# A linear-attention and two-MLP kernel: orders planned forward and backward in rounds, w2's loads held back, the last block's output tiles finished in turn

## The chip, the cores and the metric
The kernel runs on one core of a Trainium2 chip. The core has a matrix engine (TensorE, PE in the profile, with its weight loads as PEld), VectorE (DVE), ScalarE (ACT), GpSimd (POOL, unused here) and SyncE (SP), which issues every DMA of this kernel. The metric is the device time of one execution in microseconds, the median over runs.

## What is computed
```python
# q, k, v, f_logit: (4, 8, 768, 48); heads are joined to x: (3072, 384)
f = 1.0 / (1.0 + np.exp(-f_logit))
for t in range(S):
    state = f[:, :, t, :, None] * state + np.einsum('bhd,bhe->bhde', k[:, :, t], v[:, :, t])
    y[:, :, t] = np.einsum('bhd,bhde->bhe', q[:, :, t], state)
# MLP 1: w_in (384, 2048), w_out (2048, 384)
h = x @ w_in
x = (h * np.clip(h + 3.0, 0.0, 6.0) / 6.0) @ w_out
# MLP 2: weights of its own, same shapes
h = x @ w_in
out = (h * np.tanh(np.log1p(np.exp(h)))) @ w_out
```

## The kernel before
**Tiling.** The scan is done in 24 units `u` (4 batches of 6 chunks of 128 tokens): per unit the decay logs are summed (`sum_up`, matmuls with the triangle `tri`, in units 0 to 7; a scan on VectorE, L278, later), `k` is transposed (`turn`: tile `m`), `scores` are formed (tile `a`), masked by VectorE, and `values` and `outer` multiply them and update the state `st`. A unit ends with two halves of x, `xh` and `xl`: every fp32 value is carried as a rounded part and a rest, and a product takes three matmuls (high by high, low by high, high by low; `passes`).

The MLPs work on 12 blocks of 512 tokens, six for MLP 1 and six for MLP 2. A block has 16 hidden tiles f. `hidden` records for each: nine matmuls of 128x512 into a bank `h` (MLP 2 uses `h`, `a` and `m` in turn), here called H of f; the chain on VectorE and ScalarE that makes `gh` and `gl` (MLP 1: `g`, `gh`, `gl`; MLP 2: a longer chain with tiles `k` and `q`); and nine output matmuls, three for each of the tiles o0, o1, o2 (O of f). Those three banks collect over all 16 f; after f=15 ScalarE, VectorE and ScalarE copy them out and SP stores them, 256 KB each. Attention units of block j+1 are woven between the tiles of block j; units 0 to 3, and most of the preparation, stand ahead of the first hidden matmul (the head).

**Weights.** They come as 64-bit words (`raw`, 768 KB a tile). `stream` makes fp32 of them with two ScalarE passes (`we<-raw`, `raw<-raw`) and two VectorE passes (L220, L222); `weight` splits them into `wh` and `wl`. Those of MLP 1 are converted in the head and in block 0. Those of MLP 2 (w2) are converted later, stored to DRAM (`w<-we`) and read back at the start of MLP 2.

**Order.** Every operation is recorded in a `Plan` with an engine, a cost and a rank, and `emit` sets the order: it walks forward in planned time, and each engine that comes free takes the ready operation of lowest rank. The rank is a due time in hidden tiles (`i` = 16 x block + f). SP's DMAs have planned places of the same kind. In the last block the hidden matmuls of f from 2 up get a rank lower by `TAIL_LEAD` (6), so that they run ahead of the output matmuls. Where the plan leaves TensorE a gap ahead of the first hidden matmul, `emit` fills it with `warm`: matmuls of `cap` into a bank that nobody reads, as many pieces of 128 columns as fit, plus six at the very start.

Of the kernel before, what the change touches and what calls it, by code (L numbers as in the profile page):

```python
# [23 lines left out]
NF = DFF // 128  # L24
# [19 lines left out]
GAP = 0.28  # L44
HOLD, TAIL_LEAD = 14, 6
WE = 2
W2_AT = 40
W2_GAP = 3.5
SPANS = ((0, D), (HB, R))
# [24 lines left out]
class Op:  # L74
    __slots__ = ("eng", "cost", "lat", "rank", "fn", "deps", "after", "seq", "start", "end", "left", "outs", "ready")


class Plan:
# [10 lines left out]
    def op(self, eng, cost, rank, fn, r=(), w=(), lat=0.0):  # L89
        o = Op()  # L90
        o.eng, o.cost, o.lat, o.rank, o.fn, o.seq = eng, cost, lat, rank, fn, len(self.ops)
        o.deps, o.after = set(), set()
# [20 lines left out]

    def emit(self, filled, limit, unit, warm):
# [8 lines left out]
        for o in self.ops:  # L123
            o.outs, o.left, o.ready = [], 0, 0.0
        for o in self.ops:
            o.deps.discard(o)
            o.after -= o.deps | {o}
            for d in o.deps | o.after:
                d.outs.append(o)
            o.left = len(o.deps) + len(o.after)  # L130
        wait = {o.eng: [] for o in self.ops}
        free = dict.fromkeys(wait, 0.0)
        for o in self.ops:
            if not o.left:
                wait[o.eng].append(o)
        order = []
        while any(wait.values()):
            now, eng = min((max(free[e], min(o.ready for o in c)), e) for e, c in wait.items() if c)
            o = min((o for o in wait[eng] if o.ready <= now), key=lambda o: (o.rank, o.seq))
            wait[eng].remove(o)  # L140
            if eng == filled:
                limit = min(limit, now) if o.rank >= 1 else limit
                if free[eng] and free[eng] + unit < now < limit:
                    order.append(int((now - free[eng]) / unit))
            o.start, o.end = now, now + o.cost
            free[eng] = o.end
            order.append(o)
            for d in o.outs:
                t = o.start if d in o.after or o in d.after and o not in d.deps else \
                    o.end + o.lat + (GAP if d.eng != eng else 0.0)  # L150
                d.ready = max(d.ready, t)
                d.left -= 1
                if not d.left:
                    wait[d.eng].append(d)
# [681 lines left out]
```

## Time and profile before
| | |
|---|---|
| time, median of 3 runs | 894.73 us (893.9 to 894.84) |
| profiled execution | 895.67 us, span 893.9 us |
| TensorE busy | 881.0 us (99%) |
| VectorE busy | 668.7 us (75%) |
| ScalarE busy | 561.5 us (63%) |
| mean granted TensorE clock | 0.997 |

The span runs from the first to the last instruction of the profiled execution; the execution's own time has 1.77 us around it. Busy times are sums over the instructions of an engine. In the timeline a row gives start, duration, engine, line, operation, tiles (out<-in), shapes and how many instructions were joined; what ended an idle time before the row stands behind it in brackets. Matmuls overlap in the pipeline, so starts say more than durations.

### The profile page before, as it was taken

The numbers are of one execution on the slowest core, as the hardware profiler recorded it, in microseconds if no ns is written. First come the engines' busy times: TensorE is split into PE (matmuls) and PEld (weight loads), VectorE is DVE, ScalarE is ACT, GpSimd is POOL, SyncE is SP. The second block draws the span as 40 slices with busy tenths as digits, with TensorE's granted clock in tenths as the row PEclk, the third lists the DMA queues.
The fourth block names the chain that finished last, engine by engine and source line by source line (L and its number), as shares of the span: only waits on it lengthen the run. The fifth ranks groups of instructions, "written<-read, shape, count | busy, mean of one in ns | idle before, by whom it ended". The sixth has DMA issues, their size and how long they took to land.

```text
span 893.9 us, 15680 instructions
## 1 busy us (share of the span) xinstructions
PE 881.0 (99%) x6341; PEld 722.0 (81%) x6341; DVE 668.7 (75%) x1045; ACT 561.5 (63%) x978; POOL 0.2 (0%) x4
## 2 busy tenths in 40 slices
PE   9999989999999999999999999999999999999997
PEld 6878868888888888888888888888888888888785
DVE  4898999778777555653565977888878888785894
ACT  6898787667646454433545766666666667664773
POOL 0000000000000000000000000000000000000000
PEclk9999999999999999999999999999999999999999
DMA  8766656867544222100323200100100100000001
GB/s 267 237 200 225 205 192 210 267 209 234 192 133 130 65 65 76 60 25 1 120 92 102 76 1 12 59 1 24 48 0 24 48 1 18 30 1 1 36 1 40
DMA packets 32465, 83.29 MB, mean 93 GB/s; under 512 B 3712, under 2 KB 7040, under 8 KB 32384
## 3 DMA queue, kind: packets, MB, share of 16 engines
q1 hardware_dynamic: 32384, 82.20, 28.9%
q8 instruction: 52, 0.85, 0.4%
q14 instruction: 29, 0.24, 0.1%
HBM read 66.45 MB, written 15.73 MB: 92 GB/s over the span
## 4 chain that ended last, share of the span: by engine, by line
PE 93%; ACT 2%; DVE 2%; DMA 1%; issue 0%; ACTq 0%
PE o L200 45%; PE h L200 30%; PE a L200 12%; PE m L200 7%; DMA raw<-w 1%; PE m L300 1%; ACT we L187 1%; ACT wh L187 0%; DVE we L220 0%; ACT raw L187 0%; DVE b L278 0%; DVE A L290 0%; PE m L400 0%; DVE we L222 0%; ACT vk L187 0%
## 5 line engine op out<-in xcount | busy, mean ns | idle before, releaser
L200 PE MATMUL o<-gh,wh 128*128 128x512 f32 x570 | 225.1, 395 | 0.0
L200 PE MATMUL o<-gl,wh 128*128 128x512 f32 x570 | 222.3, 390 | 0.7 <-DVE gl L203 0.7
L200 PE MATMUL o<-gh,wl 128*128 128x512 f32 x570 | 222.0, 389 | 0.0
L200 PE MATMUL h<-xh,wh 128*128 128x512 f32 x402 | 159.0, 396 | 2.1 <-DVE g L517 2.1
L200 PE MATMUL h<-xh,wl 128*128 128x512 f32 x402 | 157.3, 391 | 0.3 <-DVE wl L203 0.3
L200 PE MATMUL h<-xl,wh 128*128 128x512 f32 x402 | 157.0, 391 | 0.0
L200 PEld LDWEIGHTS o<-gh,wh 128*128 128x128 f32 x570 | 107.0, 188 | 24.2 <-issue 0.4
L200 PEld LDWEIGHTS o<-gh,wl 128*128 128x128 f32 x570 | 107.0, 188 | 22.6
L200 PEld LDWEIGHTS o<-gl,wh 128*128 128x128 f32 x570 | 107.1, 188 | 22.5 <-DVE gl L203 1.1
L517 DVE SCALAR_TENSOR_TENSOR g<-g,h 128x512 f32<-128x512 f32 x96 | 65.6, 684 | 79.1 <-ACT g L187 79.0
L187 ACT ACTIVATE g<-h,small 128x512 f32<-128x512 f32 x96 | 65.8, 686 | 82.3 <-PE h L200 69.7
L187 ACT ACTIVATE gh<-q 128x512 fp32r<-128x512 f32 x94 | 59.3, 631 | 79.8 <-DVE q L206 75.0
L203 DVE TENSOR_TENSOR gl<-g,gh 128x512 fp32r<-128x512 f32 x96 | 66.1, 689 | 33.4 <-ACT gh L187 33.1
L200 PEld LDWEIGHTS h<-xh,wh 128*128 128x128 f32 x402 | 75.6, 188 | 18.7 <-DVE g L517 2.7
L200 PEld LDWEIGHTS h<-xh,wl 128*128 128x128 f32 x402 | 75.7, 188 | 17.1 <-DVE wl L203 1.0
L200 PEld LDWEIGHTS h<-xl,wh 128*128 128x128 f32 x402 | 75.8, 188 | 15.2
L187 ACT ACTIVATE q<-k,small 128x512 f32<-128x512 f32 x96 | 69.4, 723 | 28.8 <-DVE k L525 25.1
L206 DVE TENSOR_TENSOR q<-q,k 128x512 f32<-128x512 f32 x96 | 66.0, 688 | 24.9 <-ACT q L187 23.5
L187 ACT ACTIVATE gh<-g 128x512 fp32r<-128x512 f32 x96 | 60.2, 627 | 35.3 <-DVE g L517 35.2
L203 DVE TENSOR_TENSOR gl<-q,gh 128x512 fp32r<-128x512 f32 x94 | 64.7, 688 | 9.2 <-ACT gh L187 8.5
L187 ACT ACTIVATE k<-k 128x512 f32<-128x512 f32 x96 | 59.6, 625 | 17.6 <-DVE k L522 17.4
L525 DVE SCALAR_TENSOR_TENSOR k<-k 128x512 f32<-128x512 f32 x96 | 65.3, 684 | 0.7 <-ACT k L187 0.7
(140 smaller groups left out, 1164.8 us busy)
## 6 DMA issues: line engine op xcount, KB each, us to landing
raw<-w SPq DMA_DIRECT2D x32, 768.0 KB, 5.2
v<-vs SPq DMA_DIRECT2D x16, 512.0 KB, 3.8
w<-we SPq DMA_DIRECT2D x16, 384.0 KB, 2.7
raw<-w SPq DMA_DIRECT2D x16, 384.0 KB, 3.0
k<-kt SPq DMA_DIRECT2D x24, 224.0 KB, 4.3
q<-qt SPq DMA_DIRECT2D x24, 224.0 KB, 3.6
x<-o SPq DMA_DIRECT2D x18, 256.0 KB, 2.1
f<-x SPq DMA_DIRECT2D x18, 256.0 KB, 2.6
```

The source lines that it names most:

```text
L187: lambda: nc.scalar.activation(out=out(), in_=in_(), func=func, **k), r, w)
L200: nc.tensor.matmul(**k)
L203: dve(n, rank, lambda: nc.vector.tensor_tensor(out=out(), in0=a(), in1=b().bitcast(F32), op=ALU.subtract), r, w)
L206: dve(n, rank, lambda: nc.vector.tensor_tensor(out=out(), in0=a(), in1=b(), op=ALU.mult), r, w)
L300: nc.tensor.transpose(ztv()[:, p, :], k3()[:, p, :], ident[0:R, 0:R])
L517: dve(n, rank, lambda: nc.vector.scalar_tensor_tensor(out=gg(), in0=gg(), scalar=6.0, in1=zn(), op0=ALU.min, op1=ALU.mult), (g, z), (g,))
L525: dve(n, rank, lambda: nc.vector.scalar_tensor_tensor(out=ee(), in0=ee(), scalar=2.0, in1=ee(), op0=ALU.add, op1=ALU.mult), (e,), (e,))
```

## The change
1. `forward` is the old walk. `backward` walks from the planned end back and gives each operation its latest start, which becomes its rank in the next forward walk. They alternate for six rounds, and the plan with the earliest end is kept; operations are emitted by planned start.
2. Fillers in gaps that begin before 8 us of planned time are counted at twice the length, so fewer are placed.
3. w2's raw loads wait for a hidden tile: tile f for the hidden tile number 22 + 3.5 f (22 is f=6 of block 1).
4. In the last block the lead of the hidden matmuls grows in steps from 6/14 to 6. The output matmuls of f from 12 up are ranked by output tile: all of o0 first, then o1. o2 is collected up to f=13 and copied to SBUF (`rest`); f=14 and 15 are collected in two halves of 256 columns in the two `h` banks, VectorE adds `rest` to each, and each half is stored by itself (128 KB).

```diff
 GAP = 0.28
+COLD = 8.0
+ROUNDS = 6
 HOLD, TAIL_LEAD = 14, 6
+APART = 4
...
 W2_AT = 40
 W2_GAP = 3.5
+W2_FROM = 22
...
+    def forward(self):
+
+        wait = {o.eng: [] for o in self.ops}
+        free = dict.fromkeys(wait, 0.0)
+        for o in self.ops:
+            o.ready, o.left = 0.0, len(o.deps) + len(o.after)
+            if not o.left:
+                wait[o.eng].append(o)
+        while any(wait.values()):
+            now, eng = min((max(free[e], min(o.ready for o in c)), e) for e, c in wait.items() if c)
+            o = min((o for o in wait[eng] if o.ready <= now), key=lambda o: (o.rank, o.seq))
+            wait[eng].remove(o)
+            o.start, o.end = now, now + o.cost
+            free[eng] = o.end
+            for d in o.outs:
+                d.ready = max(d.ready, o.end + o.lat + (GAP if d.eng != eng else 0.0) if o in d.deps else o.start)
+                d.left -= 1
+                if not d.left:
+                    wait[d.eng].append(d)
+        return max(o.end for o in self.ops)
...
+    def backward(self):
+
+        end = max(o.end for o in self.ops)
+        wait = {o.eng: [] for o in self.ops}
+        free = dict.fromkeys(wait, end)
+        for o in self.ops:
+            o.ready, o.left = end, len(o.outs)
+            if not o.left:
+                wait[o.eng].append(o)
+        while any(wait.values()):
+            now, eng = max((min(free[e], max(o.ready for o in c)), e) for e, c in wait.items() if c)
+            o = max((o for o in wait[eng] if o.ready >= now), key=lambda o: (o.end, o.seq))
+            wait[eng].remove(o)
+            o.rank = now - o.cost
+            free[eng] = o.rank
+            for d in o.deps | o.after:
+                d.ready = min(d.ready, o.rank - d.lat - (GAP if d.eng != eng else 0.0) if d in o.deps else o.rank + d.cost)
+                d.left -= 1
+                if not d.left:
+                    wait[d.eng].append(d)
...
         for o in self.ops:
-            o.outs, o.left, o.ready = [], 0, 0.0
-        for o in self.ops:
             o.deps.discard(o)
             o.after -= o.deps | {o}
+            o.outs = []
+        for o in self.ops:
             for d in o.deps | o.after:
                 d.outs.append(o)
-            o.left = len(o.deps) + len(o.after)
...
-        order = []
...
-            if eng == filled:
-                limit = min(limit, now) if o.rank >= 1 else limit
-                if free[eng] and free[eng] + unit < now < limit:
-                    order.append(int((now - free[eng]) / unit))
...
+        best = None
+        for i in range(ROUNDS + 1):
+            end = self.forward()
+            if best is None or end < best[0]:
+                best = end, [(o, o.start, o.end) for o in self.ops]
+            if i < ROUNDS:
+                self.backward()
+        for o, o.start, o.end in best[1]:
+            pass
+        order, free = [], {}
+        for o in sorted(self.ops, key=lambda o: (o.start, o.seq)):
+            if o.eng == filled:
+                limit = min(limit, o.start) if o.mlp else limit
+                if o.eng in free:
+                    slow = unit * (2 if free[o.eng] < COLD else 1)
+                    if free[o.eng] + slow < o.start < limit:
+                        order.append(int((o.start - free[o.eng]) / slow))
+                free[o.eng] = o.end
             order.append(o)
...
-    def stream(w, f, rank, name=None):
+    def stream(w, f, rank, name=None, after=()):
         raw = new("raw", [128, 2 * DM * (2 if wide else 1)], 2, U32)
-        dma(rank - 3, raw, lambda: w[f].bitcast(U32), (), (raw,), 128 * 2 * DM * (8 if wide else 4), name)
+        dma(rank - 3, raw, lambda: w[f].bitcast(U32), after, (raw,), 128 * 2 * DM * (8 if wide else 4), name)
...
-    pso = {}
+    pso, halves, rest = {}, [], []
...
-        pe(9 * (0.0135 + n / 2400), i - TAIL_LEAD * tail, run, [("w", f, 0), ("w", f, 1), *x_keys(ph, j, 0), *x_keys(ph, j, 1)], (z,))
+        pe(9 * (0.0135 + n / 2400), i - (TAIL_LEAD * (f - NF + HOLD + 1) / HOLD if tail else 0), run, [("w", f, 0), ("w", f, 1), *x_keys(ph, j, 0), *x_keys(ph, j, 1)], (z, ("h", i)))
...
         if f == 0:
             pso[0] = [bank(f"o{m}", [128, 512], 1) for m in range(KC)]
         for m in range(KC):
-            zo = pso[0][m]
-
-            def run(m=m, zo=zo):
-                for t, (a, b) in enumerate(passes):
-                    mm(out=zo()[:, 0:n], lhsT=ww[f][a][:, DM + m * 128:DM + (m + 1) * 128], rhs=gn[b](),
-                       start=(f == 0 and t == 0), stop=(f == NF - 1 and t == 2))
-
-            pe(3 * (0.0135 + n / 2400), i + 1.5 + m * 0.01, run, (("w", f, 0), ("w", f, 1), *gs, *((zo,) if f else ())),
-               (zo,))
-            if f == NF - 1:
+            cut = tail and m == KC - 1 and f >= NF - 2
+            for i0, (s0, s1) in enumerate(((0, n // 2), (n // 2, n)) if cut else ((0, n),)):
+                if cut and f == NF - 2:
+                    halves.append(bank("h", [128, 512], 2))
+                zo = halves[i0] if cut else pso[0][m]
+                begin = f == NF - 2 if cut else not f
+                done = f == NF - 1 or tail and m == KC - 1 and f == NF - 3
+
+                def run(m=m, zo=zo, s0=s0, s1=s1, begin=begin, done=done):
+                    for t, (a, b) in enumerate(passes):
+                        mm(out=zo()[:, s0:s1], lhsT=ww[f][a][:, DM + m * 128:DM + (m + 1) * 128], rhs=gn[b]()[:, s0:s1],
+                           start=(begin and t == 0), stop=(done and t == 2))
+
+                at = i - f + NF - APART + 1.5 + (m * APART + f + 2 * i0) * 0.01 if tail and f >= NF - APART else i + 1.5 + m * 0.01
+                pe(3 * (0.0135 + (s1 - s0) / 2400), at, run, (("w", f, 0), ("w", f, 1), *gs, *(() if begin else (zo,))), (zo,))
+                if not done:
+                    continue
                 scale = 1.0 / 6.0 if ph == 1 else 1.0
-                o = new("o", [128, 512], 3)
-                on = lambda o=o: o()[:, 0:n]
-                zi = lambda zo=zo: zo()[:, 0:n]
-                if m == 1:
+                o = new("k" if cut else "o", [128, 512], 3)
+                on = lambda o=o, s0=s0, s1=s1: o()[:, s0:s1]
+                zi = lambda zo=zo, s0=s0, s1=s1: zo()[:, s0:s1]
+                if cut:
+                    dve(s1 - s0, i, lambda on=on, zi=zi, s0=s0, s1=s1: nc.vector.tensor_tensor(
+                        out=on(), in0=zi(), in1=rest[0]()[:, s0:s1], op=ALU.add), (zo, rest[0]), (o,))
+                elif m == 1:
                     dve(n, i, lambda on=on, zi=zi: nc.vector.tensor_scalar(out=on(), in0=zi(), scalar1=scale,
                                                                            scalar2=None, op0=ALU.mult), (zo,), (o,))
                 else:
                     act(n, i, on, zi, AF.Copy, (zo,), (o,), scale=scale)
+                if f < NF - 1:
+                    rest.append(o)
+                    continue
                 dst = x1_d[j] if ph == 1 else out_v[:, :, t0:t0 + n]
-                dma(i, lambda m=m, dst=dst: dst[:, m, :], on, (o,), (("x1", j, m) if ph == 1 else ("out", j, m),),
-                    128 * n * 4)
+                dma(i, lambda m=m, dst=dst, s0=s0, s1=s1: dst[:, m, s0:s1], on, (o,),
+                    (("x1", j, m) if ph == 1 else ("out", j, m, s0),), 128 * (s1 - s0) * 4)
 
 
     P.op("act", 1.3, -99, lambda: nc.scalar.preload_act_table_set("natural_log_exp_and_others"))
@@ -603,7 +657,7 @@
         for f in range(NF):
             hidden(1, j, f, 16 * j + f)
     for f in range(NF):
-        key, src = stream(w2, f, W2_AT + W2_GAP * f)
+        key, src = stream(w2, f, W2_AT + W2_GAP * f, after=(("h", int(W2_FROM + W2_GAP * f)),))
```

In the planned order this moves instructions at three places. First, TensorE at the head. `o_147` is the bank of the fillers, `o_164<-tri,f` are unit 0's sums, `m<-ident,k` a `turn` and `a<-q,k` its `scores`. Before, from the start:

```order
L200 MATMUL o_147<-cap 112x128
L200 MATMUL o_147<-cap 112x512 x3
L200 MATMUL o_147<-cap 112x128 x2
L200 MATMUL o_164<-tri,f 112x128 x4
L200 MATMUL o_147<-cap 112x512 x2
L200 MATMUL o_147<-cap 112x128 x2
L400 MATMUL m<-ident,k 128x112 x4
```

and after:

```order
L241 MATMUL o_147<-cap 112x128
L241 MATMUL o_147<-cap 112x512
L241 MATMUL o_147<-cap 112x128 x3
L241 MATMUL o_164<-tri,f 112x128 x4
L241 MATMUL o_147<-cap 112x512
L241 MATMUL o_147<-cap 112x128
L441 MATMUL m<-ident,k 128x112 x4
```

The first batch shrinks from 1,920 to 1,024 columns and the second from 1,280 to 640. Further on, up to the first hidden matmul (`h<-xh,wh_96`), 13 pieces of 128 columns become 6. Just ahead of that matmul stand before (`h<-g,v` belongs to unit 3, `m<-tri,f` to unit 5):

```order
L200 MATMUL h<-g,v 32x128 x5
L200 MATMUL m<-tri,f 112x128 x4
L200 MATMUL o_147<-cap 112x512
L200 MATMUL o_147<-cap 112x128
L200 MATMUL h<-xh,wh_96 128x512
```

and after:

```order
L241 MATMUL h<-g,v 32x128 x5
L441 MATMUL m<-ident,k 128x112 x4
L241 MATMUL a<-q,k 128x128 x8
L241 MATMUL o_147<-cap 112x128 x3
L241 MATMUL h<-xh,wh_96 128x512
```

Unit 4's `turn` and `scores`, which stood behind the nine matmuls of H0, now stand ahead of them. Before, H0, H1, unit 4's `outer` and `values` and H2 come before O0, the first output matmuls; after, H0, H1, unit 4's `outer` and `values`, and then O0.

Second, VectorE at the start of block 1 (`b<-cap,f` is a unit's scan, `we` a conversion pass, `st` and `A<-a,tri` follow a unit's scores). Before:

```order
L278 SCALAR_TENSOR_TENSOR b<-cap,f 112x512
L206 TENSOR_TENSOR k<-k,f 112x512
L290 TENSOR_TENSOR A<-q,b 64x512
L290 TENSOR_TENSOR A<-q,b 48x512
L203 TENSOR_TENSOR gl<-g,gh 128x512
L206 TENSOR_TENSOR k<-k,f 112x512
L290 TENSOR_TENSOR A<-q,b 64x512
L290 TENSOR_TENSOR A<-q,b 48x512
L220 SCALAR_TENSOR_TENSOR we<-we,raw 128x768
L329 TENSOR_TENSOR st<-st,a 112x192
L339 TENSOR_TENSOR A<-a,tri 64x256 x4
L517 SCALAR_TENSOR_TENSOR g<-g,h 128x512
```

and after:

```order
L319 SCALAR_TENSOR_TENSOR b<-cap,f 112x512
L247 TENSOR_TENSOR k<-k,f 112x512
L244 TENSOR_TENSOR gl<-g,gh 128x512
L331 TENSOR_TENSOR A<-q,b 64x512
L331 TENSOR_TENSOR A<-q,b 48x512
L247 TENSOR_TENSOR k<-k,f 112x512
L558 SCALAR_TENSOR_TENSOR g<-g,h 128x512
L331 TENSOR_TENSOR A<-q,b 64x512
L331 TENSOR_TENSOR A<-q,b 48x512
L244 TENSOR_TENSOR gl<-g,gh 128x512
L370 TENSOR_TENSOR st<-st,a 112x192
L380 TENSOR_TENSOR A<-a,tri 64x256 x4
```

The conversion pass is gone from there, and one `g` stands ahead of the second unit's work and of the masks.

Third, TensorE's end (wh_124 to wl_127 are the weights of f=14 and 15; `f` and `A` hold the last two `gh` and `gl`). Before, the three output tiles in turn for each f:

```order
L200 MATMUL o_8200<-f,wh_124 128x512 x2
L200 MATMUL o_8200<-f,wl_125 128x512
L200 MATMUL o_8207<-f,wh_124 128x512 x2
L200 MATMUL o_8207<-f,wl_125 128x512
L200 MATMUL o_8214<-f,wh_124 128x512 x2
L200 MATMUL o_8214<-f,wl_125 128x512
L200 MATMUL o_8200<-A,wh_126 128x512 x2
L200 MATMUL o_8200<-A,wl_127 128x512
L200 MATMUL o_8207<-A,wh_126 128x512 x2
L200 MATMUL o_8207<-A,wl_127 128x512
L200 MATMUL o_8214<-A,wh_126 128x512 x2
L200 MATMUL o_8214<-A,wl_127 128x512
```

and after:

```order
L241 MATMUL o_8162<-A,wh_126 128x512 x2
L241 MATMUL o_8162<-A,wl_127 128x512
L241 MATMUL o_8190<-f,wh_124 128x512 x2
L241 MATMUL o_8190<-f,wl_125 128x512
L241 MATMUL o_8190<-A,wh_126 128x512 x2
L241 MATMUL o_8190<-A,wl_127 128x512
L241 MATMUL h<-f,wh_124 128x256 x2
L241 MATMUL h<-f,wl_125 128x256
L241 MATMUL h<-A,wh_126 128x256 x2
L241 MATMUL h<-A,wl_127 128x256
L241 MATMUL h<-f,wh_124 128x256 x2
L241 MATMUL h<-f,wl_125 128x256
```

The last two rows (f=15 of the second half) are left out. o0 is complete 18 matmuls (6 full ones and 12 halves) before the end, o1 12 halves before it.

In the same block H6 moves: H1 and H6 use the one bank `m`, and between them stand 18 matmuls before (H5 and O0) and 81 after.

## Rows read from the trace of the kernel before
**Rows 1.** The page, part 1: busy us, share of the span, instructions

```profile
PE 881.0 (99%) x6341; PEld 722.0 (81%) x6341; DVE 668.7 (75%) x1045; ACT 561.5 (63%) x978; POOL 0.2 (0%) x4
```

**Rows 2.** The chain that ended last: start us, us, what

```profile
871.37 16.33 PE o L200 x72
```

**Rows 3.** TensorE's waits: us in total, times, longest

```profile
PE h L200 <- DVE g L517: 2.1, 2, 1.9
...
PE h L200 <- DVE wl L203: 0.3, 1, 0.3
```

**Rows 4.** Timeline of TensorE, head

```profile
1.59 6.41 PE L200 MATMUL o<-cap 112*112 112x128 f32 x12 [1.59 <-DVE small L573]
7.84 1.04 PE L200 MATMUL o<-tri,f 128*112 128x128 f32 x8
8.71 2.32 PE L200 MATMUL o<-cap 112*112 112x512 f32 x8
10.87 0.55 PE L400 MATMUL m<-ident,k 112*128 112x112 f32 x4
...
33.00 0.48 PE L200 MATMUL h<-xh,wh 128*128 128x512 f32 x1
...
36.72 0.50 PE L200 MATMUL h<-xh,wh 128*128 128x512 f32 x1
```

**Rows 5.** Timeline of ScalarE and VectorE, head

```profile
4.03 0.58 ACT L187 ACTIVATE f<-f 128x448 f32<-128x448 f32 x1
8.97 0.60 ACT L187 ACTIVATE f<-o 112x512 f32<-112x512 f32 x1 [4.37 <-PE o L200]
...
9.70 0.69 DVE L206 TENSOR_TENSOR k<-k,f 112x512 f32<-112x512 f32 x1 [7.56 <-ACT f L187]
```

**Rows 6.** Windows of 20 us: busy us by engine, granted clock, DMA

```profile
120.00:140.00 20.00, 18.14 (x196) 14.46 (x195) 18.19 (x32) 15.37 (x36) 0.00 (x0) 0.91 0.62 202
...
60.00:80.00 20.00, 20.00 (x163) 16.22 (x162) 18.65 (x26) 16.67 (x26) 0.00 (x0) 1.00 0.61 202
```

**Rows 7.** Timeline of TensorE, start of block 1

```profile
117.09 0.50 PE L200 MATMUL o<-gl,wh 128*128 128x512 f32 x1 [0.74 <-DVE gl L203]
...
122.72 0.50 PE L200 MATMUL h<-xh,wh 128*128 128x512 f32 x1 [1.86 <-DVE g L517]
```

**Rows 8.** Timeline of VectorE, start of block 1

```profile
109.63 0.96 DVE L220 SCALAR_TENSOR_TENSOR we<-we,raw 128x768 uint32<-128x768 uint32 x1 [0.55 <-ACT raw L187]
...
118.96 0.96 DVE L220 SCALAR_TENSOR_TENSOR we<-we,raw 128x768 uint32<-128x768 uint32 x1
119.84 0.35 DVE L329 TENSOR_TENSOR st<-st,a 112x192 f32<-112x192 f32 x1
120.22 1.73 DVE L339 TENSOR_TENSOR A<-a,tri 64x256 f32<-64x256 f32 x4
121.98 0.69 DVE L517 SCALAR_TENSOR_TENSOR g<-g,h 128x512 f32<-128x512 f32 x1
```

**Rows 9.** Timeline of TensorE, last block

```profile
836.18 0.50 PE L200 MATMUL m<-xh,wh 128*128 128x512 f32 x1 [1.35 <-DVE q L206]
```

**Rows 10.** Timeline at the end, and the DMA issues of that stretch (KB, median us to landing)

```profile
887.30 0.39 PE L200 MATMUL o<-A,wl 128*128 128x512 f32 x1
887.72 0.60 ACT L187 ACTIVATE o<-o 128x512 f32<-128x512 f32 x1 [0.76 <-PE o L200]
...
out_dram<-o SPq DMA_DIRECT2D x3, 256.0 KB, 3.8
```

**Rows 11.** Timeline of SP's queue: stores of converted w2 tiles, first and last of 14

```profile
140.13 0.34 SPq L193 DMA_DIRECT2D w<-we  x1
...
255.72 0.42 SPq L193 DMA_DIRECT2D w<-we  x1
```

**Rows 12.** The page, part 5: a group of weight loads (busy, mean ns)

```profile
L200 PEld LDWEIGHTS o<-gh,wh 128*128 128x128 f32 x570 | 107.0, 188 | 24.2 <-issue 0.4
```

**Rows 13.** The page, part 6: stores of x between the MLPs (KB, us to landing)

```profile
x<-o SPq DMA_DIRECT2D x18, 256.0 KB, 2.1
```

More of the change, by code (lines that the diff above doesn't have):

```diff
@@ L74 @@
 class Op:
-    __slots__ = ("eng", "cost", "lat", "rank", "fn", "deps", "after", "seq", "start", "end", "left", "outs", "ready")
+    __slots__ = ("mlp", "eng", "cost", "lat", "rank", "fn", "deps", "after", "seq", "start", "end", "left", "outs", "ready")
 class Plan:
@@ L91, in op @@
         o.eng, o.cost, o.lat, o.rank, o.fn, o.seq = eng, cost, lat, rank, fn, len(self.ops)
+        o.mlp = rank >= 1
         o.deps, o.after = set(), set()
@@ L123, in emit @@
         for o in self.ops:
-            o.outs, o.left, o.ready = [], 0, 0.0
-        for o in self.ops:
             o.deps.discard(o)
             o.after -= o.deps | {o}
+            o.outs = []
+        for o in self.ops:
             for d in o.deps | o.after:
                 d.outs.append(o)
-            o.left = len(o.deps) + len(o.after)
[L131 to L135, printed above, removed]
-        order = []
[L137 to L140, printed above, removed]
-            if eng == filled:
-                limit = min(limit, now) if o.rank >= 1 else limit
-                if free[eng] and free[eng] + unit < now < limit:
-                    order.append(int((now - free[eng]) / unit))
-            o.start, o.end = now, now + o.cost
-            free[eng] = o.end
-            order.append(o)
[L148 to L154, printed above, removed]
+        best = None
[16 more added lines that the diff above has]
+                free[o.eng] = o.end
+            order.append(o)
         for o in order:
```

## The prediction, made before the changed kernel ran
> **What bounds the kernel now.** I read the page's busy times first: TensorE is busy 881.0 of 893.9 us [rows 1], so the kernel is TensorE's, and a gain can come from three things only: its idle time, work that need not be done (the filler matmuls on `cap`), and matmuls that run at the slower clock. The chain that ended last says the same at the end: 72 output matmuls in 16.33 us [rows 2], 0.2268 us from start to start. That is the price of every 128x512 matmul here; 3,456 of them are 784 us and are untouched.
>
> Then TensorE's waits: six lines, the first for VectorE's `g` and the last for `wl` [rows 3], all for VectorE or ScalarE and none for a DMA. They sum to 6.6 us, a little over half of the 12.9 us of idle time; the rest is the end of the span, where TensorE has nothing left. The timeline then tells where each wait stands:
>
> - Head. TensorE starts at 1.59 with six fillers (3 of 512 columns, 3 of 128) and reaches unit 0's `tri` sums at 7.84; after these come two more long fillers, and the first `turn` starts at 10.87, the first hidden matmul (H0) at 33.00 [rows 4]. ScalarE had `f` ready at 4.03 + 0.58 = 4.61 and then waited 4.37 us for TensorE [rows 5]: a filler that counts as busy held up the chain.
> - Block 0. VectorE is busy 18.65 of 20 us at 60 to 80 us [rows 6]: little room.
> - Start of block 1. Two waits for `g`, 2.1 us together [rows 3], the longer (1.86) at 122.72, and one of 0.74 for `gl` at 117.09 [rows 7], and the granted clock is 0.91 of full over 120 to 140 us [rows 6]. The levels are 1.2 and 2.4 GHz, so 20 x 0.09 x 2 = 3.6 us ran at the lower one and cost half of that. VectorE is not slow there; its queue holds the wrong things: two passes of w2's conversion (0.96 us each, the first at 109.63) stand before one `g`, a third at 118.96 before the masks, and the `g` that frees the bank for the next hidden tile comes last, at 121.98 [rows 8].
> - Last block. H6 waits 1.35 us for bank `m`, which VectorE's multiply into `q` frees [rows 9].
> - Tail. The last matmul starts at 887.30, its eviction at 887.72 takes 0.60, and the store issued then takes about 3.8 us [rows 10]. That is 6.2 us from the last matmul's end to the span's.
>
> **The sum.** It is made against the profiled run (895.67 us, of which 1.77 lie around the span).
>
> *Head.* The first batch of fillers loses 512 + 384 − 896 columns: before it is 1,920 columns in 7.84 − 1.59 = 6.25 us, after 1,024, so 3.33 us: `tri` starts at 4.9 instead of 7.84, just after `f` (4.61). It runs at the lower level then, 2 x 0.87 us, to 6.7. ScalarE's and VectorE's steps behind it gave `k` at 9.70 + 0.69 = 10.39 [rows 5], 1.68 after `tri`'s end at 8.71; so they give it at 8.3 to 8.4, and the first `turn` starts at about 8.5 instead of 10.87. The second batch of fillers is 640 columns instead of 1,280 (2.16 us at the full level); begun at 6.7, it ends at about 8.3 if the clock rises at 7.84 as before. That is −2.4. Between there and H0 the fillers shrink from 13 to 6 pieces of 128 columns, each 2.16/10 = 0.216 us: −1.5. But unit 4's `turn` and `scores` now stand ahead of H0. They take 36.72 − 33.00 − 9 x 0.2268 = 1.7 us [rows 4]. So H0 starts near 30.7 (−2.3), and H1, which no longer has them before it, 3.9 us earlier. Bounds: −3 (their inputs come late) to −5 (all fillers were in the way). **−3.9.**
>
> *New wait at O0.* TensorE now reaches O0 two hidden tiles after H0, with unit 3's sums between them: about 36.9. VectorE has between unit 3's `xl` (about 30.3) and `gl` of f=0: five conversion or `wl` passes at 0.88 from start to start (118.96 to 119.84 [rows 8]), two masks, `g`, `gl` and `xl` of about 0.6, and two small ones of 0.35: some 7.8 us, so about 38.1. Wait 1.2, less the old wait for `wl` (0.3 in the list, 0.4 by starts): **+0.8**, bounds 0 and +2 (a wait as long as the 1.86 of [rows 7]).
>
> *Start of block 1.* No w2 conversion stands there any more, and `g` is moved ahead of the masks, whose scores come from TensorE itself. What TensorE lost: 2.1 + 0.7 by the list, and 1.8 by the lower clock: **−4.6**, bounds −2.8 (the waits go, the lower clock stays) and −5.2 (each wait's start-to-start gap is 0.1 to 0.25 longer than its number).
>
> *Conversions in blocks 1 to 4.* Each of the 16 tiles brings two VectorE passes and two ScalarE passes, one tile every 3.5 hidden tiles (3.5 x 18 x 0.2268 = 14.3 us of matmuls, so the passes take an eighth of it). In before 14 of the 16 tiles were stored between 140 and 256 us [rows 11], and no wait of TensorE stands between 130 and 830 us: there is cover. Where a unit's scan and masks fall together with a conversion, a short wait can come back: **+0.3**, bounds 0 and +4.6 (all of what block 1 loses now).
>
> *Last block.* In the order of after, 81 matmuls (18 us) instead of 18 (4.1 us) stand between H1 and H6, the two users of bank `m`; VectorE needs under 6 us for H1's chain. **−1.4**, bounds −1.0 and −1.5. The stepwise leads also let 57 matmuls (12.9 us) stand between the last hidden tile and its first output matmul, where 63 (14.3 us) stood; no output matmul of the last block waited before, so I count nothing, and +1.4 as the bound.
>
> *Tail.* o0 and o1 are finished 2.7 and 1.4 us before the last matmul (12 halves, 6 x 0.2268). The last eviction has 256 columns a row: VectorE's four 256-wide masks take 1.73, so 0.43 each [rows 8] against 0.60: −0.17. The 12 half matmuls cost at least half of 0.2268, and at most 0.188, the length of a weight load [rows 12]: nothing to +0.9. Eight `tri` pieces of 128 columns start every 0.11 us [rows 4], so the weight load isn't the bound even there; I take 0.12, +0.1. The last store has 128 KB. Stores of 256 KB that go out at other times land in 2.1 us [rows 13], the last three, which overlap, in 3.8. With o0 and o1 out of the way I take 2.6: −1.2. **−1.3**, bounds +0.9 (the store as slow as before) and −1.9.
> The Trainium skill (DMA: Bandwidth & Descriptors, "Anatomy of one DMA") speaks against this: about 2.0 us of a transfer are fixed, and only bytes at 436 GB/s scale, which would make halving worth 0.3 us and the tail −0.4 if overlap cost nothing. The 2.1 against 3.8 us for one size say that overlap does cost here, so the measurement decides for now; by the rule alone the sum would be 0.9 smaller.
>
> Sum: −3.9 + 0.8 − 4.6 + 0.3 − 1.4 − 1.3 = −10.1, so 885.6 for a profiled run. The median of the timed runs is 0.94 below the profiled one, which makes **884.6**. Its own range, with terms erring independently, is 882 to 887.3.
>
> **Rivals.**
> *B: block 0 eats the head.* VectorE is 93% busy there [rows 6] and does the same conversions in the same block. If its work from H0 to the end of block 0 can't start earlier, the 3.1 us of head and O0 are given back as waits inside block 0: −7.0, 887.7. For it: the busy share. Against: conversions for block 0 do not wait for TensorE, and VectorE's order puts every `gl` before work that is due later.
> *C: the conversions carry their waits along* to blocks 1 to 4: +4.6 instead of +0.3, so 888.9. For it: the same passes. Against: the gap of 14 us between tiles, and the 14 tiles that were converted without a wait. B and C together: 892.
> *D: w2's loads block SP's queue.* They now wait for a hidden tile, and SP issues in order: the units' `q`, `f`, `k`, `v` loads stand behind each of the 16 waiting loads. If they come late, TensorE waits for attention. This decides above 10.1/16 = 0.63 us for each gate; at 0.9 us the kernel is at 884.6 + 14.4 = 899. Against: no DMA in TensorE's waits now, and the loads behind a gate feed work one or more groups away.
> *E: only what the page calls idle comes back.* 12.9 less 1.6 at the start and 6.2 at the end leaves 5.1 inside; with the tail's 1.3 that is −6.4, 888.3. Against: fillers and half-speed matmuls count as busy, so more can be had.
>
> **How the numbers follow.** My case 0.65, B 0.13, C 0.06, B with C 0.02, E 0.05, D 0.09 (two thirds of it slower, a third near the point where it decides). A run of this kernel can tell about 0.2% (1.8 us) from no change, which leaves faster 0.91, same 0.03, slower 0.06. The range must reach B, C and E, so its upper end is 889.6; its lower end takes in most of the better bounds (head −5, block 1 −5.2, tail −1.9, no new waits): 881.0. Left out are D, B with C, and the tips of my case.
>
> **What would show it.** Right: first hidden matmul at about 30.7; granted clock 1.00 at 120 to 140 us; no wait for bank `m` in the last block; wait at O0 of about 1 us; 5 us from last matmul to end. Wrong: TensorE waits for `gl` all through block 0 (B); waits of over 1 us, with a lower clock, in blocks 1 to 4 (C); lines of TensorE waiting for DMA, or VectorE and ScalarE waiting for `q`, `k`, `f` (D); a last store that still takes 3.8 us.

## The result and the profile after
The changed kernel takes 884.23 us (median of six runs, 883.81 to 886.52) against 893.78 us before on the same chip: ratio 0.9897, 95% interval 0.9883 to 0.9910. The forecast was 884.6, in a range of 881.0 to 889.6. The profiled execution took 885.92 us, its span is 884.2 us, so it is one of the slower of the six; this matters below. One execution of one kernel below, the profiled one of the held-back loads alone, ran at a granted clock of 0.528 throughout (1653.37 us) and is left out.

The page's busy times:

```profile
PE 873.2 (99%) x6333; PEld 719.8 (81%) x6333; DVE 669.1 (76%) x1047; ACT 564.2 (64%) x978; POOL 0.2 (0%) x4
```

TensorE's busy time fell by 7.8 us [rows 1] although no needed matmul was taken out: fillers, and the longer time of matmuls at the lower clock, count as busy. Its waits (us in total, times, longest):

```profile
PE m L441 <- DVE k L247: 2.1, 3, 1.2
PE o L241 <- DVE small L627: 1.6, 1, 1.6
PE o L241 <- DVE gl L244: 1.0, 1, 1.0
```

All the waits of block 1 and the one of the last block [rows 3, 7, 9] are gone, and so are the small ones for `kn` and `wl`; new are three waits of `turn` for `k` in the head, and one for `gl`. The timeline of TensorE, head and first wait:

```profile
1.59 3.53 PE L241 MATMUL o<-cap 112*112 112x128 f32 x10 [1.59 <-DVE small L627]
4.96 1.04 PE L241 MATMUL o<-tri,f 128*112 128x128 f32 x8
5.83 1.24 PE L241 MATMUL o<-cap 112*112 112x512 f32 x4
7.56 0.60 PE L441 MATMUL m<-ident,k 112*128 112x112 f32 x4 [0.48 <-DVE k L247]
...
21.66 0.57 PE L441 MATMUL m<-ident,k 112*128 112x112 f32 x4 [1.25 <-DVE k L247]
...
32.37 0.48 PE L241 MATMUL h<-xh,wh 128*128 128x512 f32 x1
...
40.18 0.50 PE L241 MATMUL o<-gl,wh 128*128 128x512 f32 x1 [1.04 <-DVE gl L244]
```

Against [rows 4] the first `turn` starts 3.3 us earlier, but the first hidden matmul only 0.6 us earlier. Of the 2.7 us between, unit 4's `turn` and `scores`, now ahead of H0, take 1.6, and seven filler pieces fewer give back about as much. Most of the rest is late `k`, above all unit 3's: by the starts of matmuls its wait (at 21.66) costs 1.3 us, unit 4's (at 30.10) 0.4, and the `scores` right behind the first take 1.6 us instead of 1.1. The chain through the head, and VectorE's row for unit 3's `k`:

```profile
11.08 9.64 DMA k<-kt
```

```profile
20.82 0.69 DVE L247 TENSOR_TENSOR k<-k,o 112x512 f32<-112x512 f32 x1 [2.79 <-DMA k<-kt]
```

A load of 224 KB took 9.64 us to land, and VectorE stood still for it for 2.79 us. Start of block 1 by windows (busy us of PE, PEld, DVE, ACT, POOL, granted clock, DMA share, GB/s), and H6 of the last block:

```profile
120.00:140.00 20.00, 20.00 (x212) 16.21 (x214) 14.16 (x25) 14.79 (x32) 0.00 (x0) 1.00 0.39 123
```

```profile
830.95 0.39 PE L241 MATMUL m<-xh,wh 128*128 128x512 f32 x1
```

The granted clock is 1.00 there, against 0.91 in [rows 6], and H6 has no wait, against 1.35 us in [rows 9]. The end, by timeline, with the DMA issues (KB, median us to landing) and the issue times of the two half stores (ns, min/median/max):

```profile
877.82 0.28 PE L241 MATMUL h<-A,wl 128*128 128x256 f32 x1
...
877.95 1.49 SPq L234 DMA_DIRECT2D out_dram<-k  x2
...
878.14 0.42 DVE L599 TENSOR_TENSOR k<-h,o 128x256 f32<-128x256 f32 x1 [0.22 <-PE h L241]
```

```profile
out_dram<-o SPq DMA_DIRECT2D x2, 256.0 KB, 3.7
out_dram<-k SPq DMA_DIRECT2D x2, 128.0 KB, 3.0
```

```profile
L234 SPq DMA_DIRECT2D out_dram<-k x2: 384/700/1017, 877.9 to 879.1; - x2
```

From the start of the last matmul to the end of the span it is 884.2 − 877.82 = 6.4 us, against 893.9 − 887.30 = 6.6 in [rows 10]. Behind its last store SP tests `flag` and branches over the general path; only then come its eight waits for what is still under way. Its branch and these waits, before and after (ns, first and last start):

```profile
L768 SPq COMPARE_BRANCH  x1: 53/53/53, 888.7 to 888.7; - x1
L768 SPq EVENT_SEMAPHORE  x8: 17/17/17, 892.0 to 892.6; - x8
```

```profile
L822 SPq COMPARE_BRANCH  x1: 53/53/53, 879.5 to 879.5; - x1
L822 SPq EVENT_SEMAPHORE  x8: 17/17/17, 882.3 to 882.8; - x8
```

Set side by side by the starts of hidden tiles (H0 of block 0, 1, 2, the first of the last block) the 9.7 us come from (us):

| stretch | before | after | gained | forecast |
|---|---|---|---|---|
| start to H0 of block 0 | 33.00 | 32.37 | 0.6 | 2.3 |
| H0 of block 0 to H0 of block 1 | 80.35 | 78.05 | 2.3 | 0.8 (1.6 moved ahead, 0.8 lost) |
| block 1 | 82.99 | 78.17 | 4.8 | 4.6 |
| block 2 to the last block's first tile | 617.90 | 617.88 | 0.0 | −0.3 |
| that tile to the last matmul's start | 73.06 | 71.35 | 1.7 | 1.4 |
| from there to the end of the span | 6.6 | 6.38 | 0.2 | 1.3 |

### The profile page after: what moved, and what is told of

Its sections match the earlier page's. It is cut to its first block, busy times and chain, and to the rows that moved or that the text cites. A ratio compares the mean times of both kernels' runs of the same rounds, so it can differ in the third digit from the quotient of the medians.

```text
span 884.2 us, 15685 instructions
## 1 busy us (share of the span) xinstructions
PE 873.2 (99%) x6333; PEld 719.8 (81%) x6333; DVE 669.1 (76%) x1047; ACT 564.2 (64%) x978; POOL 0.2 (0%) x4
## 4 chain that ended last, share of the span: by engine, by line
PE 95%; DVE 2%; DMA 2%; SPq 0%; issue 0%; DVEq 0%
PE o L241 45%; PE h L241 31%; PE a L241 12%; PE m L241 7%; DMA k<-kt 2%; PE m L341 1%; DVE we L261 0%; SPq L234 0%; DVE we L263 0%; DVE A L429 0%; DVE wl L244 0%; DVE xl L244 0%; DVE q L247 0%; DVE k L247 0%; PE m L441 0%
## 5 line engine op out<-in xcount | busy, mean ns | idle before, releaser
L228 ACT ACTIVATE gh<-g 128x512 fp32r<-128x512 f32 x96 | 60.2, 627 | 20.8 <-DVE g L558 20.1
```

The costliest lines, as they stand in the source:

```text
L228: lambda: nc.scalar.activation(out=out(), in_=in_(), func=func, **k), r, w)
```

## The experiments
The theory under test (A): the gain is made of TensorE's waits and half-speed stretches in four separate places, each with its own cause. Its rivals: one part of the change is the whole gain (B: the held-back loads; C: the rounds); the held-back loads block SP's queue; the last block's wait belongs to the lead's step as such; the halves make the tail shorter by the store's size. A letter means what the expectation beside it says. Times are compared by the ratio to the kernel before, run on the same chip each time.

**The loads of w2 free again.** Edit to the changed kernel:
```diff
-        key, src = stream(w2, f, W2_AT + W2_GAP * f, after=(("h", int(W2_FROM + W2_GAP * f)),))
+        key, src = stream(w2, f, W2_AT + W2_GAP * f)
```


> The change with w2's raw loads free again (no wait for a hidden tile), rounds kept. In the planned order no w2 conversion comes back to the start of block 1. Theory A (the waits of block 1 come from w2's conversion passes standing in VectorE's queue there, and planning in rounds keeps them away by itself): within 0.5 us of the change, about 884. Rival B (holding the loads back is what did it, through the queue of SP or DMA traffic): the 4.6 us or so come back, about 889.

Measured: 884.63 us, 0.9895 (0.9880 to 0.9909), the same as the change. B falls: with rounds the held-back loads add nothing that can be measured.

**One forward walk.** `ROUNDS = 0`, all else as in the change.

> The change with one forward walk (no rounds), loads still held back. No w2 conversion stands at the start of block 1 here either. Theory A: block 1 stays without its waits, and only the head's reordering (unit 4's turn and scores ahead of the first hidden matmul, one wait for kn) is lost, +0.5 to +1.5 us: about 885 to 886. Rival C (the rounds are the gain): most of it is lost, 889 or more.

Measured: 887.41 us, 0.9924 (0.9911 to 0.9936). C falls, yet A's +0.5 to +1.5 was too small: it is about +2.5 to 3. Two places hold it. From H0 of block 0 to H0 of block 2 the profile has 158.32 us against 156.22 in the change (unit 4's `turn` and `scores` behind H0, and the wait for `kn`, less the wait at O0); as H0 itself comes at 30.88, 1.5 us before the change's, 0.6 of this is lost. And the end is slower: 7.6 us from the last matmul's start (878.70) to the end of the span (886.3).

```profile
877.59 1.09 ACT L228 ACTIVATE o<-o 128x512 f32<-128x512 f32 x2 [5.01 <-PE o L241]
...
878.37 0.42 DVE L599 TENSOR_TENSOR k<-h,o 128x256 f32<-128x256 f32 x1 [1.45 <-PE h L241]
...
878.70 0.81 SPq L234 DMA_DIRECT2D out_dram<-o  x2
```

In that order the third tile's first part is finished after o0, and ScalarE takes the two copies one behind the other at 877.59: the stores of o0 and o1 go out only at 878.70, with the halves right behind. So cutting the tile without finishing the others early costs 1 us at the end instead of saving any (6.6 before).

**Neither.** Both edits together.

> Neither rounds nor held-back loads; fillers, lead in steps and the cut tail kept. Two passes of w2's conversion stand before the g at the start of block 1 again, as before the change. Theory A: the waits at block 1 come back with the lower clock behind them, +4.5 to +5.5 us over the forward-only kernel: about 890. Rivals B and C need only the one part that each names; if A is wrong the time is that of one of the two single runs.

Measured: 891.84 us, 0.9973 (0.9961 to 0.9986): 4.4 us above the forward-only kernel, where 4.5 to 5.5 was expected; its runs spread from 890.25 to 895.68. TensorE's waits, the window, and a conversion pass and the late `g` in VectorE's queue:

```profile
PE h L241 <- DVE g L558: 1.9, 1, 1.9
...
PE o L241 <- DVE gl L244: 0.7, 1, 0.7
```

```profile
120.00:140.00 20.00, 20.00 (x267) 15.92 (x271) 17.01 (x28) 14.54 (x31) 0.00 (x0) 0.91 0.65 211
```

```profile
116.23 0.96 DVE L261 SCALAR_TENSOR_TENSOR we<-we,raw 128x768 uint32<-128x768 uint32 x1
...
119.25 0.69 DVE L558 SCALAR_TENSOR_TENSOR g<-g,h 128x512 f32<-128x512 f32 x1
```

The two waits of [rows 7] are back to the tenth of a microsecond (the short second one for `g` in [rows 3] is not), and so is the clock of 0.91 behind the longer one. From H0 of block 1 to H0 of block 2 the profile has 83.01 us, against 78.21 in the forward-only one and 82.99 before. The two kernels differ in when w2's conversions come, and in what the plan shifts for them.

**The held-back loads alone**, in the kernel before:
```diff
-        pe(..., i - TAIL_LEAD * tail, run, [...], (z,))
+        pe(..., i - TAIL_LEAD * tail, run, [...], (z, ("h", i)))
...
-        key, src = stream(w2, f, W2_AT + W2_GAP * f)
+        key, src = stream(w2, f, W2_AT + W2_GAP * f, after=(("h", int(22 + W2_GAP * f)),))
```


> The kernel before with w2's held-back loads alone. No w2 conversion stands at the start of block 1; fillers, head, the last block (18 matmuls between the users of bank m) and the tail are as before. Theory A: it takes the 4.5 to 5.2 us of block 1 and nothing else, so 0.9940 to 0.9950 of the time before, with the wait of 1.35 us for bank m still there. Rival D (held-back loads block SP's queue): the gain is smaller or lost, and TensorE waits at the gates in blocks 1 to 4.

Measured: 889.92 us, 0.9953 (0.9939 to 0.9967), 4.1 us faster than before, a little less than expected, with 0.9940 to 0.9950 inside the interval. So by the times the loss of block 1 can be taken away by either part; it is counted once. Whether the wait of 1.35 us is still there was not seen, as this kernel has no profile that can be read beside the others. D (SP's queue blocked by loads that wait) has nothing for it: the time falls, and no other profile with held-back loads has a wait of TensorE in blocks 1 to 4.

**The last block's lead as one step.**
```diff
-i - (TAIL_LEAD * (f - NF + HOLD + 1) / HOLD if tail else 0)
+i - TAIL_LEAD * tail
```


> The change with the last block's lead as one step of 6 again. 36 matmuls (8.2 us) stand between H1 and H6, the users of bank m, where the bank came free 5.4 us after H1 before the change. Theory A (the wait for bank m is set by the distance alone): no wait, within 0.5 us of the change. Rival D (the step itself brings the wait, whatever the distance): +1.4 us, about 885.6.

Measured: 884.91 us, 0.9902 (0.9887 to 0.9916), the same. H6 follows without a wait:

```profile
824.64 0.39 PE L241 MATMUL m<-xh,wh 128*128 128x512 f32 x1
```

The step itself does not bring the wait; with the rounds 36 matmuls stand between the two users of bank `m`, where 18 stood, and that is enough. TensorE's list of instructions in the head is the same as the change's, and shows what an earlier landing does:

```profile
18.56 0.69 DVE L247 TENSOR_TENSOR k<-k,o 112x512 f32<-112x512 f32 x1 [0.52 <-DMA k<-kt]
```

```profile
30.20 0.47 PE L241 MATMUL h<-xh,wh 128*128 128x512 f32 x1
```

VectorE starts unit 3's `k` 2.3 us earlier than in the change, and H0 comes 2.2 us earlier.

**The fillers as before.** `COLD = 0.0`.

> The change with the fillers of the first 8 us counted once again, so 1,920 and 1,280 columns as before instead of 1,024 and 640; the rest of the head as after. Theory A (the fillers stood in unit 0's way and the first turn starts some 2.3 us later with them): the loads that follow get that much more time, so a wait for them that the change has (up to 2.8 us on VectorE for unit 3's k) is hidden again, and the loss is smaller than 2.3: +1 to +2 us against the change. Rival F (the head is set by the loads alone): within 0.4 us of the change.

Measured: 885.52 us, 0.9901 (0.9884 to 0.9918). By time neither theory is settled, as this median can't be told from the change's. The profile:

```profile
10.47 0.55 PE L441 MATMUL m<-ident,k 112*128 112x112 f32 x4
...
32.60 0.48 PE L241 MATMUL h<-xh,wh 128*128 128x512 f32 x1
```

The first `turn` starts within 0.4 us of where it did before, and no wait for `k` is left; H0 at 32.6 stands against a mean of 31.5 over seven profiles with few fillers and the change's order of TensorE's head (30.2, 30.9, 31.4, 31.7, 32.0, 32.1, 32.4). So 2 to 3 us at the first `turn` are worth about 1 at H0 as a mean. Where few fillers met a `k` in time (the third tile whole, below: first `turn` at 8.62, no wait, H0 at 30.87), 1.9 us at the first `turn` were worth 1.7 at H0, by these two profiles.

**The change again**, beside the next kernels.

> The change itself once more, beside the three kernels of this group. If the head's time varies with how fast its loads land, as the earlier profiles suggest (first hidden matmul between 30.2 and 32.4 us with one order of instructions), it will stand anywhere in that band here too, and the median within 1 us of 884.2 to 885.

Measured: 884.71 us, 0.9893 (0.9878 to 0.9908); H0 at 32.12. Unit 3's `k` by SP's issue, its time to landing (us, last number) and VectorE's row:

```profile
10.79 0.33 SPq L234 DMA_DIRECT2D k<-kt  x1
...
k<-kt SPq DMA_DIRECT2D x1, 224.0 KB, 9.7
...
20.57 0.69 DVE L247 TENSOR_TENSOR k<-k,o 112x512 f32<-112x512 f32 x1 [1.86 <-ACT raw L228]
```

The row names ScalarE's pass on `raw`, which this instruction does not read and which ends at the same moment. The load lands at 10.79 + 9.7 = 20.5, 0.1 us before VectorE starts, as it does in the profiles whose row names the load (20.7 and 20.82 in the change).

**Unit 3's `k` and `q` ahead of the first weight tile** in the list of first loads:
```diff
-... v1 w0 k2 q2 v2 k3 q3 w1 v3 w2
+... v1 k2 q2 v2 k3 q3 w0 w1 v3 w2
```


> The change with the first weight tile's load (768 KB) moved behind unit 3's k and q in the list of the first loads. Theory A (in the head the DMA engines are full and unit 3's k is late behind that tile): k lands some us earlier, VectorE no longer waits for it, and the first hidden matmul comes 0.5 to 1.5 us earlier, unless the weight tile becomes the late one. Rival G (the weight tile is on the path to the first hidden matmul as closely): no gain, or a loss of up to 2 us.

Measured: 883.98 us, 0.9882 (0.9865 to 0.9898), with one run at 887.63 that is also the profiled one. `k` is in time, but TensorE then waits 0.8 us at O0 for ScalarE's `gh` and 1.1 for `gl`, and the granted clock falls behind these waits, which fits the 887.63:

```profile
42.00:44.00 2.00, 2.00 (x11) 1.88 (x10) 2.00 (x4) 2.00 (x4) 0.00 (x0) 0.50 0.96 389
```

Inconclusive by time.

**The third tile whole.**
```diff
-            cut = tail and m == KC - 1 and f >= NF - 2
+            cut = False
...
-                done = f == NF - 1 or tail and m == KC - 1 and f == NF - 3
+                done = f == NF - 1
```


> The change with the third output tile of the last block whole again: one store of 256 KB, ScalarE's eviction, no halves, o0 and o1 still finished first. By the prediction's step (halving is worth 0.17 of eviction and 1.2 of the store): +1.3 us. Rival H (halves overlap the stores of o1 and of each other, so the last one lands no sooner than a whole one would): within 0.4 us of the change.

Measured: 885.28 us, 0.9900 (0.9883 to 0.9917): no difference to the change that can be told. The end by the trace:

```profile
876.21 0.39 PE L241 MATMUL o<-A,wl 128*128 128x512 f32 x1
876.64 0.60 ACT L228 ACTIVATE o<-o 128x512 f32<-128x512 f32 x1 [2.80 <-PE o L241]
```

From the last matmul's start to the end of the span (882.8) it is 6.6 us, as before. The six profiles with halves and rounds and SP's queue have 5.9 to 6.4 (mean 6.1). So against this one profile the halves are worth some 0.4 us, not 1.3, and finishing o0 and o1 early without them nothing.

**The last half from ScalarE's queue.**
```diff
+                if cut and s0:
+                    P.op("act", 0.45, i, lambda ...: nc.scalar.dma_start(out=dst[:, m, s0:s1], in_=on()), (o,), ...)
+                    continue
```


> The change with the store of the last half issued from ScalarE's queue. In the profile of the change SP needed 1.02 us to issue the first half, and the second went out 0.5 us after its data was ready. Theory A (that issue is a cost of the halves): -0.3 to -0.5 us. Rival: the landing alone counts and the gain is under 0.1 us.

Measured: 886.65 us, 0.9910 (0.9895 to 0.9926): no gain by time, and the highest ratio of the kernels with rounds; why is open. In the one profile, of a run of 885.88, VectorE waited 2.35 us for `k` and H0 came at 31.96. The end took 5.9 us from the last matmul's start, inside the 5.9 to 6.4 of the halves, so A's 0.3 to 0.5 us is not shown.

**Both edits of the tail:** the store as above, and the copy of the third tile's first part on VectorE.
```diff
-                elif m == 1:
+                elif m == 1 or not f == NF - 1:
```


> The change with two edits at the end: the copy of the third tile's first part goes to VectorE, so that ScalarE's copy of o0, and its store, is 0.6 us earlier; and the last half is stored from ScalarE's queue. Theory A (the tail's gain was lost to overlapping stores and to SP's queue): 0.4 to 0.7 us less from the last matmul to the end than the change, which has 6.26 us there. Rival: the landing of a store costs the same whenever it goes out: less than 0.2 us.

Measured: 884.13 us, 0.9887 (0.9872 to 0.9903). The four stores at the end:

```profile
874.87 2.47 SPq L234 DMA_DIRECT2D out_dram<-o  x2
...
877.45 0.36 SPq L234 DMA_DIRECT2D out_dram<-k  x1
...
878.17 0.38 ACTq L611 DMA_DIRECT2D out_dram<-k  x1
...
DMA to landing us min/median/max: 2.0/2.1/2.2
```

All four land in 2.0 to 2.2 us, halves and whole tiles alike, and the end takes 883.1 − 877.40 = 5.7 us. Against the repeat of the change that ran beside it (884.0 − 877.68 = 6.3) it is 0.6 shorter, the size that A had. A's reason is not shown by it: the last three stores (877.0, 877.45, 878.17) are in flight together here too, and the last one has landed at 880.3, 2.8 us before the end. What comes last is ScalarE, which branches at 879.1, goes on at 882.3 and is waited for by SP.

**The same with the loads' order** of the kernel further up.

> The former kernel with the first weight tile's load behind unit 3's k and q as well. If the loads' order is worth something, it is 0.5 to 1.5 us faster than the kernel without that edit, beside which it runs; if the weight tile is as close to the path, it is the same or up to 1 us slower.

Measured: 883.70 us, 0.9885 (0.9870 to 0.9901), runs from 883.21 to 884.13; the change beside it 884.71 (884.09 to 885.76), the kernel without the loads' order 884.13. So that order is worth 0.4 us here, a little less than the 0.5 to 1.5 of the expectation and not clear of noise. Against the change it is some 0.1% faster, and the intervals of the two ratios overlap: a likely gain, not a sure one. Its end takes 5.7 us too (881.4 − 875.69). Its profile has the shortest waits inside the span:

```profile
PE m L441 <- DVE k L247: 0.5, 1, 0.5
PE o L241 <- DVE gl L244: 0.4, 1, 0.4
```

## Why the prediction was right, point by point
The total was right, 9.7 of 10.1 us in the profiled spans, and so were the cause and size of its largest term. That it came within half a microsecond is luck in part: head and tail gave 1.7 and 1.1 us less than their terms in the table, and block 0 gave 1.5 more. The prediction's rival E (888.3) lies 4 us above the measured time. Of the five signs of being right three came (the clock of 1.00, no wait for bank `m`, a wait of 1 us at O0); H0 at 30.7 and 5 us from the last matmul to the end did not. (Three slips in its text: the first clause of the head's term should say that 896 columns fewer are streamed, 1,920 to 1,024; what lies between H1 and O0 is unit 4's `outer` and `values`; and the items of VectorE's stretch ahead of O0 add up to 8.1 us, not 7.8, which is also what it took, from 31.34 to 39.44.)

- **Start of block 1**, −4.6: measured −4.8 in the change, 4.4 between two kernels that differ in it (4.8 by starts), 4.1 by the loads alone. That it was VectorE's order there is shown: put the conversions back, and the two longer waits with the same clock return; let the loads go free but keep the order, and they don't. What the prediction did not say is that two parts of the change each remove it.
- **Head**, −3.9 (H0 at 30.7): in the profiled execution H0 came at 32.4, and H1 2.2 us earlier than before. The step that failed is the one that took the inputs as given: the bound "their inputs come late" was named, at 0.9 us, and was worth more. The first `turn` even came at 7.56 instead of 8.5, since `tri` already ran at the full level. But the DMA engines are full from 5 to 20 us in both kernels, and pulling TensorE forward ran into unit 3's `k`. Seven profiles with one order of TensorE's head (us):

  | profile | first `turn` | `k` lands | VectorE starts it (idle before) | H0 | from there to H0 |
  |---|---|---|---|---|---|
  | the change | 7.56 | 20.7 | 20.82 (2.79) | 32.37 | 11.55 |
  | last half from ScalarE's queue | 7.65 | 20.3 | 20.42 (2.35) | 31.96 | 11.54 |
  | lead as one step | 7.94 | 18.5 | 18.56 (0.52) | 30.20 | 11.64 |
  | both edits of the tail | 8.46 | 20.1 | 20.14 (1.58) | 31.70 | 11.56 |
  | loads free | 8.62 | 19.7 | 19.82 (1.11) | 31.37 | 11.55 |
  | the change again | 8.62 | 20.5 | 20.57 (1.86) | 32.12 | 11.55 |
  | third tile whole | 8.62 | 17.8 | 18.63 (none) | 30.87 | 12.24 |

  In six of them VectorE starts 0.1 us behind the landing and H0 follows 11.5 to 11.6 us later, whenever the first `turn` came: the spread of H0 is the landing's. In the seventh the load is in time, and H0 comes at 30.87 behind a first `turn` at 8.62, where the sum had 30.7 behind 8.5. So the sum was right for a punctual load, as far as one profile shows it. That no DMA stood in TensorE's waits before was true and misled: with the long fillers the same load had landed well before it was needed, at 17.4 before and at 17.5 with the fillers as before.
- **New wait at O0**, +0.8: 1.04 us of waiting came, the old 0.3 for `wl` went, as forecast.
- **Block 0** gave back nothing (the prediction's rival B falls). It gained another 0.6 us (0.8 by starts) that the sum left out: one wait for `kn` was in the list of six but was never placed in the timeline. Forward-only kernels still have it, so the rounds took it away. A further 0.4 of the stretch is the short wait for `g` just ahead of block 1's H0, which the sum counted with block 1.
- **Conversions in blocks 1 to 4**, +0.3: no wait came (the prediction's C and D fall).
- **Last block**, −1.4: −1.7 by the table, and the mechanism of distance is borne out: 36 matmuls between the two users of bank `m` are enough too, with the lead as one step.
- **Tail**, −1.3: measured 0.2 in the change, about 0.5 as a mean of the profiles with halves. The step that failed is the one that let the last store's landing set the end. Before, that store went out at 888.3 and landed 3.8 us later, at 892.2, but SP, which had branched at 888.7, went on only at 892.0 and went through its eight waits by 892.6 without a stop: the landing held up nothing. From SP's first wait to the end it is 1.9 us before and after (893.9 − 892.0, 884.2 − 882.3). In the change the last half landed after 2.9 us, at 882.0, and SP went on at 882.3. From SP's branch to its first wait it took 2.5 to 3.8 us in 13 profiles; how much of that is the branch and how much the landing no run separates. The 2.6 us taken for the landing were also too few: the halves took 3.0, and the first half's issue 1.02 us instead of 0.33. That the four stores crowd each other is not shown as the reason: in the kernel with unit 3's `k` first they stand as close, SP issues both halves in 0.33 us, they land after 2.3, and the end takes 6.1 all the same.
- On the halves' worth the Trainium skill (DMA: Bandwidth & Descriptors, "Anatomy of one DMA — SWDGE (gpsimd) path") was nearer than the row: by its mostly fixed 2 us halving is worth an estimated 0.3. It states this for DMAs that GpSimd issues; these are issued by SP and ScalarE. The kernel with both edits of the tail agrees that most of it is fixed, with 2.0 to 2.2 us for 128 and 256 KB alike.

What stays open: why the load lands at 17.8 in one execution and at 20.7 in another. Over 5 to 20 us the full DMA engines moved 283 GB/s in the change, 316 in the kernel with the third tile whole and 324 before, and mostly the load is later where this is lower; what sets it no run shows.

## What to carry to other kernels
Look for each wait's cause in the queue of the engine that is waited for: here the same waits could be taken away by planning or by holding a load back, and doing both paid once. Before pulling an engine forward at the start of a kernel, ask when the loads of the steps that follow land, and repeat the profile: one order of instructions had its first hidden matmul anywhere from 30.2 to 32.4. Give every line of the list of waits a place in the timeline, the small ones too. And before pricing the last store of a kernel, read what its engine does next: here a branch stood there that the landing ran beside.

## What was not expected of the hardware
- In the windows' rows the granted clock reads 1.00 in the first 5 us, although the first 1,024 filler columns took 3.37 us (1.59 to 4.96) and the later 640 at most 1.25 us (5.83 to 7.56, less 0.48 of waiting), 2.0 ns a column against 3.3. Only the spacing of the matmuls shows the lower level there:

```profile
0.00:5.00 5.00, 3.41 (x11) 2.33 (x12) 1.05 (x6) 2.53 (x4) 0.20 (x4) 1.00 0.51 149
```

- The rise comes at different moments in one order of instructions: unit 0's `tri` took 0.87 us from 4.96 in the change, and 1.70 us from 5.14 in the kernel with free loads, TensorE having been busy from 1.59 in both.
- A 224 KB load took 9.6 us to land while the DMA engines were full, and VectorE's wait for it varied between profiles of one order from none to 2.8 us.
- SP needed 0.33 us to issue a store, and 1.02 us for one that followed two others closely; in one profile of the same order at the end it needed 0.33 there too.
- From SP's taken branch at the kernel's end to its next instruction it took 3.2 us before (888.8 to 892.0), although what its first wait was for had long landed.
